# GEGLU feed-forward block: the order of the first fetches on two issue queues, and the place of ScalarE's table load

## Chip, cores and metric

The kernel runs on one core of one Trainium2 chip. The metric is the device time of one execution in microseconds (us). Before the change the median of three runs is 273.84 us (273.46 to 274.38).

## What is computed

```python
# x (32, 32, 1024); w_gate, w_up (1024, 3584); w_down (3584, 1024); all bfloat16
def reference(x, w_gate, w_up, w_down):
    return (_gelu(x @ w_gate) * (x @ w_up)) @ w_down      # gelu in its tanh form
```

With the first two dimensions of x joined there are 1024 tokens of width 1024, and 3584 hidden columns.

## The kernel before

Both matrix stages use one level of a Strassen scheme (its Winograd form). The operands are cut into two by two blocks, and seven block products replace eight, at the price of sums of blocks on VectorE and GpSimd. In the first stage the four blocks on one side are the upper and the lower 512 rows of `w_gate` (a11, a12) and of `w_up` (a21, a22). On the other side stand four blocks of x transposed: b11 and b21 (width rows 0 to 511 and 512 to 1023, tokens 0 to 511), b12 and b22 (the same rows, tokens 512 to 1023). Hidden columns are done in tiles of 128, and each product of a tile with 512 tokens is four matmuls, one for each 128 rows of width.

One of the seven products, a12 times b21, needs no sums. It is therefore computed ahead for the first 24 hidden tiles, in six groups of four tiles (group 0 to 5), and its results are copied to SBUF (`ahead`). While this runs, the rest of x and the first blocks of the weights arrive. This change concerns what groups 0 and 1 read.

**Transposed x.** Rows 0 and 1 of b21 (a row here is 128 rows of width) do not come from a transposing DMA. They are fetched untransposed into `x_nat`, as two blocks of 128 columns of x for all 512 tokens: x's first block (L199, on SyncE's queue) and x's second block (L218, on ScalarE's queue). TensorE transposes each block (`transposed`, L263, four transposes), and VectorE copies the result from PSUM into b21 (L271). Rows 2 and 3 of b21 come from a DMA transpose (L222, in `load_xT`). A one-element copy on GpSimd (L221), which reads x's first block and writes into rows 2 and 3, holds that transpose until x's first block has landed.

**Gate rows.** `load_ahead(i, k0, k1, eng)` (L204) fetches rows k0 to k1-1 of a12 for group i, 128 KB a row, on SyncE's queue unless ScalarE's is named. So "gate row k of group i" is one [128 x 512] block of `w_gate`.

**Order on TensorE** (written out by hand in the source): six warm-up products on constants (L254); four transposes of x's first block; seven short filler products on constants (L275); gate row 0 of group 0 (eight matmuls of 256 tokens, `by_halves(0)`); four transposes of x's second block; row 0 of group 1 for three tiles; row 1 of group 0 (`by_halves(1)`); row 1 of group 1 and the rest of its row 0; rows 2 and 3 of group 0 (L345 to L348); rows 2 and 3 of group 1; then groups 2 to 5, between which the first real products of the main loop begin.

**Order on the issue queues.** SyncE issues, in this order: x's first block; row 0 of group 0; row 0 of group 1; rows 2 and 3 of group 0 in one fetch; the transpose for b21 (after L221); rows 2 and 3 of group 1; two fetches for group 2; one for group 3; then w_up, w_gate, group 4, and the transposes of b11, b12 and, after group 5, b22. ScalarE issues: a small `probe` fetch (L202); x's second block; row 1 of group 0; row 1 of group 1. Behind them stands a one-column Gelu (L250), whose result nobody reads. It makes ScalarE load its table early. ScalarE's next work after that is the first copy of an `ahead` tile (L348).

The program has eight completion semaphores for these fetches, which it takes in turn. The ninth fetch in the program's order therefore waits until the first has landed, and so on.

Of the kernel before, what the change touches and what calls it, by code (L numbers as in the profile page):

```python
# [8 lines left out]
ACT = mybir.ActivationFunctionType  # L9
# [4 lines left out]
def kernel(  # L14
# [20 lines left out]
    nc = tc.nc  # L35
    P = nc.NUM_PARTITIONS
    fp32 = mybir.dt.float32
    f32r = mybir.dt.float32r
    bf16 = mybir.dt.bfloat16
# [7 lines left out]
    NB = 512  # L47
    assert N == 2 * NB and D == 2 * NB and F % (4 * P) == 0
    DT, FT = D // P, F // P
    KD = DT // 2  # L50
# [4 lines left out]
    KQ = DT // 4  # L55
# [19 lines left out]
    ework = one.enter_context(tc.tile_pool(name="ework", bufs=2))  # L75
# [62 lines left out]
    def load_w_all(ci, which):  # L138

        alloc_w(ci, which)  # L140
        load_w(nc.sync, ci, which, 0, KD if which == 0 and a12_stays(ci) else DT)
# [42 lines left out]
    ident = xpool.tile([P, P], bf16, name="ident")  # L184
# [6 lines left out]
    with tc.manual_schedule():  # L191
        def load_nat(eng, dt, p0, p1):
            eng.dma_start(
                out=x_nat[:, p0:p1, dt * P : (dt + 1) * P],
                in_=xf[p0 * P : p1 * P, (KD + dt) * P : (KD + dt + 1) * P].rearrange("(b p) d -> p b d", p=P),
            )
# [7 lines left out]
        def load_ahead(i, k0, k1, eng=nc.sync, j0=0, j1=KB):  # L204
            f0 = i * KB
            eng.dma_start(
                out=a12_ahead[i][:, k0:k1, j0 * P : j1 * P],
                in_=wg_r[:, KD + k0 : KD + k1, (f0 + j0) * P : (f0 + j1) * P],
            )

        def load_xT(nb, d0, d1):
            t = ((b11, b12), (b21, b22))[d0 // KD][nb]
            nc.sync.dma_start_transpose(
                out=t[:, d0 % KD : (d1 - 1) % KD + 1, :], in_=xf[nb * NB : (nb + 1) * NB, d0 * P : d1 * P]
            )

        load_ahead(0, 0, 1)
        load_nat(nc.scalar, 1, 0, NB_P)  # L218
        load_ahead(1, 0, 1)
        load_ahead(0, KQ, KD)  # L220
        nc.gpsimd.tensor_copy(b21[:1, KQ, :1], x_nat[:1, 0, :1])  # L221
        load_xT(0, KD + KQ, DT)  # L222
        load_ahead(0, 1, KQ, nc.scalar)
        load_ahead(1, 1, KQ, nc.scalar)
        a12_ahead += [spool.tile([P, KD, KB * P], bf16, name="a12b", tag=t) for t in ("s2", "s4", "s1", "s3")]
        load_ahead(1, KQ, KD)
        def load_halves(i):
# [12 lines left out]
        load_xT(1, KD, DT)  # L240
        for which in (1, 0):
            load_w_all(1, which)

        def gelu(src, tag, bufs):
            h = ework.tile([P, NB], bf16, name=tag, tag=tag, bufs=bufs)[:, : src.shape[-1]]
            nc.scalar.activation(h, src, ACT.Gelu_apprx_tanh)  # L246
            return h


        gelu(ident[:, :1], "h0", 6)  # L250

        warm_ps = acc("A")
        for _ in range(NWARM):
# [63 lines left out]
        def first_product(ft):  # L317
            psa = acc("A")
            prod(psa, quads(*chunk_of(ft))[0], b11, True)
            if ft < NAHEAD:  # L320
                return psa, gelu(added(ahead_at[ft], psa), "h0", 6)
            return psa, snap(psa, "sn1", 4)
# [38 lines left out]
        tt(t2, b22, t1, SUB)  # L361
        group_ahead(5, "CCAA", between=lambda: nc.scalar.copy(b22r, b22))
        begun = {ft: (psa, gelu(c, "h0", 6)) for ft, (psa, c) in begun.items()}
        tt(t3, b22, b12, SUB)
        next(chunk0)
# [8 lines left out]
        for ci in range(NCH):  # L374
# [8 lines left out]
            sn5, sn2, h1, h0 = [], [], [], []  # L383
# [17 lines left out]
            if fts[-1] < NAHEAD:  # L401
                h0 = first
# [228 lines left out]
```

## Time and profile before

| | us |
|---|---|
| median of three runs | 273.84 (273.46 to 274.38) |
| the profiled execution | 273.33 |
| its span, first to last instruction | 271.4 |
| the rest of it, around the span | 1.93 |
| TensorE busy in the span | 268.0 |
| ScalarE busy in the span | 115.4 |
| VectorE busy in the span | 204.0 |

Engines in the profile are PE (TensorE matmul), PEld (TensorE weight load), DVE (VectorE), ACT (ScalarE), POOL (GpSimd) and SP (SyncE); a name with a q at its end, such as ACTq, is an engine's instruction stream where it issues transfers. A row of the timeline gives the start and the length in us, the engine, the source line, the operation, the tile written and the tiles read, the number of instructions merged into the row, and in brackets the idle time before it with what ended it. Matmuls overlap, and their ends are modelled, so the step from one start to the next tells more than a length. A row of the list of transfers gives what is fetched, the issuing engine, the number, the size, and the time from the start of the issue until the transfer has landed.

### The profile page before, as it was taken

The numbers are of one execution on the slowest core, as the hardware profiler recorded it, in microseconds if no ns is written. First come the engines' busy times: TensorE is split into PE (matmuls) and PEld (weight loads), VectorE is DVE, ScalarE is ACT, GpSimd is POOL, SyncE is SP. The second block draws the span as 40 slices with busy tenths as digits, with TensorE's granted clock in tenths as the row PEclk, the third lists the DMA queues.
The fourth block names the chain that finished last, engine by engine and source line by source line (L and its number), as shares of the span: only waits on it lengthen the run. The fifth ranks groups of instructions, "written<-read, shape, count | busy, mean of one in ns | idle before, by whom it ended". The sixth has DMA issues, their size and how long they took to land.

```text
span 271.4 us, 3431 instructions
## 1 busy us (share of the span) xinstructions
PE 268.0 (99%) x1219; PEld 193.7 (71%) x1219; DVE 204.0 (75%) x205; ACT 115.4 (43%) x189; POOL 120.8 (45%) x61
## 2 busy tenths in 40 slices
PE   8999999999999999999999999999999999999996
PEld 5544776886787788688688687764458888888884
DVE  1447999986976877887777478469999999988711
ACT  2435756545644653645636535434000307870000
POOL 1080089997994994995995996000000000000000
PEclk9999999999999999999999999999999999999999
DMA  7999321514505505415234190005981537875111
GB/s 193 316 209 228 100 62 56 157 35 119 157 0 155 156 2 155 126 28 157 73 84 119 47 331 8 0 2 178 356 279 60 156 115 248 269 194 181 52 64 60
DMA packets 56657, 35.88 MB, mean 132 GB/s; under 512 B 10048, under 2 KB 56640, under 8 KB 56640
## 3 DMA queue, kind: packets, MB, share of 16 engines
q1 hardware_dynamic: 53232, 33.17, 43.3%
q10 hardware_dynamic: 3408, 2.49, 2.9%
q8 instruction: 10, 0.16, 0.3%
q14 instruction: 7, 0.06, 0.1%
HBM read 31.72 MB, written 2.10 MB: 125 GB/s over the span
## 4 chain that ended last, share of the span: by engine, by line
PE 99%; DVE 0%; issue 0%
PE psA L279 38%; PE psA L435 24%; PE psC L279 19%; PE psC L435 7%; PE psA L290 5%; PE psC L290 3%; PE psC L599 1%; PE psA L254 1%; PE psA L275 0%; PE tp L266 0%; DVE o_last L600 0%
## 5 line engine op out<-in xcount | busy, mean ns | idle before, releaser
L279 PE MATMUL psA<-t,s 128*128 128x512 f32 x224 | 57.2, 397 | 0.0
L246 ACT ACTIVATE h<-c 128x512 bf16<-128x512 f32 x56 | 34.4, 629 | 41.5 <-DVE c L309 41.5
L279 PEld LDWEIGHTS psA<-t,s 128*128 128x128 f32 x224 | 42.1, 188 | 9.5
L165 POOL TENSOR_TENSOR s<-wu 128x1024 fp32r<-128x1024 bf16 x13 | 29.5, 2271 | 28.0 <-DMA wu<-in_w_up_dram 24.0
L166 POOL TENSOR_TENSOR s<-s,wg 128x1024 fp32r<-128x1024 f32 x14 | 32.0, 2285 | 15.2 <-PE psA L279 14.2
L279 PE MATMUL psA<-b,wg 128*128 128x512 bf16 x128 | 29.4, 380 | 0.0
L168 POOL TENSOR_TENSOR s<-wg,wu 128x1024 fp32r<-128x1024 bf16 x13 | 28.9, 2219 | 0.0
L279 PE MATMUL psA<-t,a22r 128*128 128x512 f32 x112 | 27.9, 391 | 0.0
L279 PE MATMUL psC<-t,s 128*128 128x512 f32 x112 | 27.9, 391 | 0.0
L279 PE MATMUL psC<-b22r,s 128*128 128x512 f32 x112 | 27.7, 389 | 0.0
L309 DVE TENSOR_TENSOR c<-sn,psA 128x512 f32<-128x512 f32 x32 | 21.8, 682 | 6.7 <-PE psA L279 6.1
L314 ACT COPY sn<-psC 128x512 f32<-128x512 f32 x28 | 16.3, 588 | 22.8 <-PE psC L279 14.9
L279 PEld LDWEIGHTS psC<-t,s 128*128 128x128 f32 x112 | 21.0, 188 | 4.5
L279 PEld LDWEIGHTS psA<-t,a22r 128*128 128x128 f32 x112 | 21.0, 188 | 4.5
L279 PEld LDWEIGHTS psC<-b22r,s 128*128 128x128 f32 x112 | 21.0, 188 | 4.4
L309 DVE TENSOR_TENSOR c<-sn,psC 128x512 f32<-128x512 f32 x28 | 19.0, 686 | 6.0 <-PE psC L279 6.0
L412 DVE TENSOR_TENSOR lo<-c,h 128x512 bf16<-128x512 f32 x14 | 22.5, 1605 | 0.9
L279 PEld LDWEIGHTS <-wg 128*128 128x128 bf16 x128 | 11.8, 98 | 15.3 <-issue 2.4
L167 POOL TENSOR_TENSOR s<-wg,s 128x1024 fp32r<-128x1024 bf16 x10 | 21.6, 2160 | 0.8
L314 ACT COPY sn<-psA 128x512 f32<-128x512 f32 x32 | 18.3, 592 | 4.9 <-PE psA L279 4.6
L309 DVE TENSOR_TENSOR c<-ahead,psA 128x512 f32<-128x512 f32 x24 | 16.4, 686 | 3.5 <-PE psA L279 2.1
L412 DVE TENSOR_TENSOR hi<-c,h 128x512 bf16<-128x512 f32 x14 | 17.6, 1257 | 0.9
(88 smaller groups left out, 375.5 us busy)
## 6 DMA issues: line engine op xcount, KB each, us to landing
wu<-in_w_up_dram SPq DMA_DIRECT2D x14, 512.0 KB, 4.1
wdb<-in_w_down_dram SPq DMA_DIRECT2D x12, 512.0 KB, 4.8
wg<-in_w_gate_dram SPq DMA_DIRECT2D x10, 512.0 KB, 5.3
wdb<-in_w_down_dram SPq DMA_DIRECT2D x12, 384.0 KB, 4.5
v<-in_w_down_dram SPq DMA_DIRECT2D x4, 512.0 KB, 6.1
out_dram<-o_sb ACTq DMA_DIRECT2D x15, 128.0 KB, 1.7
v<-in_w_down_dram SPq DMA_DIRECT2D x4, 384.0 KB, 7.5
a12b<-in_w_gate_dram SPq DMA_DIRECT2D x4, 256.0 KB, 4.2
```

Source lines behind the costliest of these rows:

```text
L165: yield engs[0].tensor_tensor(s1, a21, a22, ADD)
L166: yield engs[1].tensor_tensor(s2, s1, a11, SUB)
L167: yield engs[2].tensor_tensor(s4, a12, s2, SUB)
L168: yield engs[3].tensor_tensor(s3, a11, a21, SUB)
L246: nc.scalar.activation(h, src, ACT.Gelu_apprx_tanh)
L254: nc.tensor.matmul(warm_ps, lhsT=ones_w, rhs=ones_m, start=True, stop=True)
L279: nc.tensor.matmul(ps, lhsT=lhs[:, k, :], rhs=rhs[:, k, :], start=(start and k == 0), stop=(k == KD - 1), skip_group_check=True,)
L290: nc.tensor.matmul(ps[:, cols], lhsT=a12_ahead[i][:, k, j * P : (j + 1) * P], rhs=b21[:, k, cols], start=(k == 0 and not cols.start), stop ...
L309: tt(t, s, ps, ADD)
L314: nc.scalar.copy(t, ps)
L412: tt(g_of(ft)[:, NB:], added(sn5[fl], psa[fl]), h1[fl], MUL)
L435: nc.tensor.matmul(banks[m], lhsT=lhs(k)[:, m * P : (m + 1) * P], rhs=rhs(k), start=(start and k == 0), stop=(k == HF - 1), skip_group_che ...
```

## The change

The dummy Gelu with its table load moves up on ScalarE, to stand between the probe and x's second block. Row 1 of group 0 moves from ScalarE's queue to SyncE's, ahead of the transpose for b21. Rows 2 and 3 of group 0 move from SyncE's queue to the end of ScalarE's. SyncE's first three fetches stay where they were.

```diff
         load_nat(nc.sync, 0, 0, NB_P)
         nc.scalar.dma_start(out=probe, in_=wg_r[::4, KD:, :2])
...
+        def gelu(src, tag, bufs):
+            h = ework.tile([P, NB], bf16, name=tag, tag=tag, bufs=bufs)[:, : src.shape[-1]]
+            nc.scalar.activation(h, src, ACT.Gelu_apprx_tanh)
+            return h
+
+        gelu(ident[:, :1], "h0", 6)
         load_ahead(0, 0, 1)
+        load_ahead(1, 0, 1)
         load_nat(nc.scalar, 1, 0, NB_P)
-        load_ahead(1, 0, 1)
-        load_ahead(0, KQ, KD)
+        load_ahead(0, 1, KQ)
+        load_ahead(1, 1, KQ, nc.scalar)
+        load_ahead(0, KQ, KD, nc.scalar)
         nc.gpsimd.tensor_copy(b21[:1, KQ, :1], x_nat[:1, 0, :1])
         load_xT(0, KD + KQ, DT)
-        load_ahead(0, 1, KQ, nc.scalar)
-        load_ahead(1, 1, KQ, nc.scalar)
...
-        def gelu(src, tag, bufs):
-            h = ework.tile([P, NB], bf16, name=tag, tag=tag, bufs=bufs)[:, : src.shape[-1]]
-            nc.scalar.activation(h, src, ACT.Gelu_apprx_tanh)
-            return h
-
-
-        gelu(ident[:, :1], "h0", 6)
```

In the built program the order of instructions on TensorE, VectorE and GpSimd is the same as before. On ScalarE the order is now: probe, table load, dummy Gelu (it waits for GpSimd's `ident`), x's second block, row 1 of group 1, rows 2 and 3 of group 0. Since the semaphores are taken in turn, the fetch of row 1 of group 1 now also waits until x's first block has landed, and the fetch of rows 2 and 3 of group 0 until row 0 of group 1 has landed. On SyncE the first `w_up` fetch now waits for the landing of the b21 transpose (before: of row 0 of group 1), and the `w_gate` fetch behind it for rows 2 and 3 of group 1 (before: row 1 of group 1).

## The prediction

> **What bounds the kernel now.** I read first the busy times and the chain that ended last, then TensorE's timeline of the first 14 us, then the fetches' landing times, and last the waits up to 60 us.
>
> ```profile
> PE 268.0 (99%) x1219; PEld 193.7 (71%) x1219; DVE 204.0 (75%) x205; ACT 115.4 (43%) x189; POOL 120.8 (45%) x61
> ...
> PE 99%; DVE 0%; issue 0%
> ```
>
> The span is 271.4 us. TensorE is busy for 268.0 of it, and 99% of the chain is TensorE's. In the waits of TensorE up to 14 us one row stands, the 0.8 us before its first product; from 12 to 60 us there is none of its matmul stream. So the change can gain only where TensorE's order itself gets shorter, and it touches none of TensorE's instructions. It can lose wherever a fetch lands after TensorE needs it. The work is to set landing times beside times of need.
>
> TensorE's timeline and its weight loads:
>
> ```profile
> 0.77 2.72 PE L254 MATMUL psA<-const-bfloat16-1.0 128*128 128x512 bf16 x6 [0.77 <-PEq L615]
> 3.23 0.42 PEld L266 LDWEIGHTS <-x_nat 128*128 128x128 bf16 x4 [0.64 <-DMA x_nat<-in_x_dram]
> 4.35 1.29 PEld L290 LDWEIGHTS <-a12a 128*128 128x128 bf16 x8
> 5.31 0.40 PE L290 MATMUL psC<-b,a12a 128*128 128x256 bf16 x2
> 5.66 0.32 PEld L266 LDWEIGHTS <-x_nat 128*128 128x128 bf16 x4
> 5.99 0.81 PE L290 MATMUL psA<-b,a12a 128*128 128x512 bf16 x3
> 6.64 0.38 PE L290 MATMUL psC<-b,a12a 128*128 128x256 bf16 x2
> 8.59 1.03 PE L290 MATMUL psC<-b,a12a 128*128 128x512 bf16 x4
> ```
>
> Times of need, a weight load standing 0.1 to 0.2 us ahead of its matmul: x's first block 3.23; row 0 of group 0 4.35; x's second block 5.66; row 0 of group 1 5.9; row 1 of group 0 6.5; row 1 of group 1 7.3 (four products of 0.22 us after 6.64, less the load); rows 2 and 3 of group 0, with the b21 transpose, about 8.4.
>
> ScalarE's timeline, then five transfers:
>
> ```profile
> 0.73 0.44 ACTq L202 DMA_DIRECT2D probe<-in_w_gate_dram  x1
> 1.20 0.45 ACTq L193 DMA_DIRECT2D x_nat<-in_x_dram  x1
> 1.69 1.01 ACTq L206 DMA_DIRECT2D a12a<-in_w_gate_dram  x2
> 2.73 1.28 ACT L246 ACT_TABLE_LOAD   x1 [2.73 <-issue]
> 4.02 0.21 ACT L246 ACTIVATE h<-ident 128x1 bf16<-128x1 bf16 x1
> 9.22 0.58 ACT L348 COPY ahead<-psC 128x512 f32<-128x512 f32 x1 [5.00 <-PE psC L290]
> ```
> ```profile
> x_nat<-in_x_dram SPq DMA_DIRECT2D x1, 128.0 KB, 2.4
> x_nat<-in_x_dram ACTq DMA_DIRECT2D x1, 128.0 KB, 3.3
> a12a<-in_w_gate_dram SPq DMA_DIRECT2D x1, 128.0 KB, 3.1
> a12a<-in_w_gate_dram SPq DMA_DIRECT2D x1, 256.0 KB, 4.2
> b<-in_x_dram SPq DMA_TRANSPOSE x1, 4.1
> ```
>
> Start of issue plus these times gives the landings of before: x's first block 0.74 + 2.4 = 3.1; its second 1.20 + 3.3 = 4.5; row 0 of group 0 1.24 + 3.1 = 4.3; row 0 of group 1 1.80 + 3.8 = 5.6; row 1 of group 0 1.69 + 3.7 = 5.4; row 1 of group 1 2.24 + 3.7 = 5.9; rows 2 and 3 of group 0 2.27 + 4.2 = 6.5; the transpose 3.44 + 4.1 = 7.5; rows 2 and 3 of group 1 4.83 + 4.2 = 9.0 (needed about 10.2). All are in time. Tightest are row 0 of group 0 (4.3 for 4.35) and row 0 of group 1 (5.6 for 5.9).
>
> **The change, part by part.**
>
> *Table load ahead of x's second block.* ScalarE ends the probe's issue at 1.17. Table load 1.28 and dummy Gelu 0.21 (its input `ident` is ready at 1.30, by GpSimd's rows) give 1.20 + 1.28 + 0.21 = 2.69. The second block is then issued at 2.70 instead of 1.20, 1.50 later. Its flight lies between 2.4 (the first block, nothing ahead of it) and 3.3 (the second, beside three fetches): landing at 5.1 to 6.0, against a need at 5.66. The stall is 0 to 0.34 us. I take the middle by bytes. In slices of 0.3 us, transfers begin at 1.8 to 2.1, some 1.2 after the first issue, and from 3.0 to 5.7 the core moves 283 to 372 GB/s. Some 3.9 is thus when data of the second block can start. By then SyncE's three gate rows ahead (131 KB each, 0.4 us apiece at 310 GB/s, from 2.7) are nearly through. The first block took 0.75 us for its bytes (155 and 240 GB/s in its main slices) and landed 0.4 after them: 3.9 + 0.75 + 0.4 = 5.1, with a share given to the neighbours 5.4. **Stall: 0.**
>
> The Trainium skill, "ScalarE: Activation LUTs", section "What ACT_TABLE_LOAD costs", speaks against this edit: it counts a drain of about 1.38 us to each table load of 1.28. The trace agrees with the load (1.28); between it and the work around it only 0.01 to 0.03 us stand. By the page the second block would be issued at about 4.1, which is the third rival.
>
> *Gate rows of both groups on SyncE.* SyncE's issues at 0.74, 1.24 and 1.80 stay. The fourth, at 2.27, becomes row 1 of group 0 (0.58 later than from ScalarE). With ScalarE's three fetches gone from the start, each row passes fewer bytes: row 0 of group 0 has 131 KB fewer ahead, 0.4 us, so it lands near 3.9; row 0 of group 1 near 4.3; row 1 of group 0 near 4.7 (5.5 by its old flight of 3.7 less 0.4), for 6.5. Their gain is nothing here: the seven fillers hold TensorE until about 4.4 whatever lands. Row 1 of group 1 is issued at about 3.2 (behind the second block, when x's first has landed at 3.1) and lands, with its old 3.7, at 6.9 at the latest, for 7.3. **Sum 0.** The DMA transpose still waits for L221 at 3.44, so its issue does not move.
>
> *Rows 2 and 3 of group 0, last on ScalarE.* They now wait for row 0 of group 1, at 4.3 (5.6 at worst, its old landing). Nothing is queued behind them on ScalarE until the copy at 9.22. Issued at 4.3, with data from 5.5, they share the engines with the transpose and with rows 2 and 3 of group 1 (issued 4.83). At half of some 280 GB/s, 262 KB take 1.9 us, plus 0.4: 7.8. Upper bound: last of the three, they land where rows 2 and 3 of group 1 land now, 9.0, or a little after, at 9.2. Need 8.4, so the price is 0 to 0.8 us; by the flight of the same size now, 4.3 + 4.2 = 8.5, it is 0.1. I take **0**, being nearer to the shared case: bytes issued ahead are 1.05 MB with the transpose, fewer than the 1.31 MB that now land by 7.5.
>
> The Trainium skill, "DMA: Bandwidth & Descriptors", section "Issuing engines are not separate DMA queues", says that fetches of all issuing engines run on the same 16 engines and interleave, so that a second queue saves only issue time. By it the fetch takes the 4.2 of its neighbours, 8.5, and the sum would be 0.1 more.
>
> *Later fetches.* `w_up` waits for the transpose (about 7.2 instead of an issue at 6.99), `w_gate` for rows 2 and 3 of group 1 (about 9.0; its issue now runs from 7.53 to 9.23). Both stand behind 1.5 MB still to be moved, 5 us at 300 GB/s, so the engines do not starve. The nearest need is b22: landed at 25.9, its sum on VectorE ends at 28.25 and TensorE uses it from 29.6. That spare 1.35 us covers what shift is left, at most 0.5.
>
> **Sum.** 273.33 + 0 + 0 + 0 = 273.33 against the profiled execution. This one lies 0.5 us below the median of the runs; on the median the forecast is **273.8 us, no change**. What a measurement of this kernel can tell from no change is about 0.3%, 0.8 us.
>
> **Rivals.**
>
> 1. *Late fetches* (22%). The second block takes 3.3 (0.3 us), or rows 2 and 3 of group 0 fall behind the transpose (0.1 to 0.8). For it: needs 5.66 and 8.4 lie inside both ranges. Against: fewer bytes in front. Time 274.1 to 274.6, both together 274.9.
>
> 2. *A gain from spare time* (12%). Row 0 of group 0 now lands with 0.05 us to spare, so runs in which it is late stall and the new order frees them: 273.84 to 273.46 are the median and the fastest run, so about 0.4, 273.4; with the other tight row up to 272.9. Against: the profiled execution has no such stall.
>
> 3. *Slower: ScalarE's queue is held longer* (10%). Place: between the dummy Gelu and the second block's issue. What follows a Gelu at once there is not shown before, as ScalarE's next work comes at 9.22. Each us by which the issue passes 5.66 - 2.4 = 3.26 is a us of stall at 5.66; from 4.1 on it exceeds 0.8 us and decides. An issue at 4.1 lands at 6.5 to 7.4: +0.8 to +1.7, 274.6 to 275.6. Against: near the end an output is issued 0.03 us after ScalarE's cast of it.
>
> 4. *A stall keeps TensorE slow* (4%). Products of 256 tokens start about 0.21 us apart up to 5.31 and 0.11 after, while the page's granted clock reads 9 in every slice. If a stall at 5.66 put this step off, each further us of slow stretch costs half a us: 274.4 to 275.0. The Trainium skill, "TensorE: Matmul & The Clock Gate", Part 1, has such a gate with a free-running window; that its phase differs by run fits the spread of 0.9 us.
>
> 5. *The change does less than it says*: two of SyncE's rows stood there already, and only row 1 of group 0 joins them. That gives the forecast's own time.
>
> **Chances and range.** Forecast 52%, rivals 22, 12, 10 and 4. Beyond 0.3% slower (over 274.66) lie most of rival 3, half of rival 4 and a fifth of rival 1: 15%. Faster than 273.02: a third of rival 2 and the runs' spread, 7%. Within: 78%. The range, 273.0 to 274.9, takes in the unknown prices of rival 1 and most of rival 2, and leaves out the rest of rivals 3 and 4.
>
> **What the changed profile would show.** ScalarE's table load at 1.2, x's second block issued at 2.7 and landed by 5.6; the weight loads of L266's second row with no idle time that a DMA ended; rows 2 and 3 of group 0 issued near 4.3 and landed before 8.4; TensorE's share still 99%. A wait of TensorE for `x_nat` or `a12a` between 5 and 9 us would prove me wrong by its length, and an issue of the second block after 3.3 would be rival 3.

## The result

The changed kernel takes 275.06 us (median of 22 executions, 273.38 to 277.05) against 273.56 us for the kernel before (22 executions, 272.76 to 274.38). The ratio is 1.0064, with a 95% interval from 1.0048 to 1.0080. It is slower, by about 1.5 us, where no change was forecast, and the median lies above the range given. The profiled execution of the changed kernel took 275.14 us, with a span of 273.3 us: 1.9 us more than the span of before.

In the page, TensorE has lost its hold on the chain:

```profile
PE 268.9 (98%) x1219; PEld 193.9 (71%) x1219; DVE 202.7 (74%) x205; ACT 115.9 (42%) x189; POOL 119.5 (44%) x61
...
PE 95%; DMA 3%; SPq 0%; DVE 0%; issue 0%
```

The chain in order of time, from the start up to 16 us (start, length, what), says which transfers stand in it:

```profile
1.24 0.51 SPq L206
1.75 0.05 issue
1.80 3.44 DMA a12a<-in_w_gate_dram
5.24 0.02 issue
5.26 5.12 DMA a12a<-in_w_gate_dram
10.38 0.05 issue
10.43 1.04 PE psC L288 x4
```

The first transfer is row 0 of group 1, from SyncE's queue. The second is rows 2 and 3 of group 0, issued 0.02 us after the first has landed. TensorE starts on them 0.05 us after they have landed. So one fetch waits for another, and TensorE waits for the second. Its timeline and ScalarE's (line numbers are two lower than before) show the same from the engines:

```profile
5.39 0.63 PE L288 MATMUL psC<-b,a12a 128*128 128x256 bf16 x2
6.25 0.63 PE L264 MATMUL tp<-ident,x_nat 128*128 128x128 bf16 x4
7.37 0.38 PE L288 MATMUL psC<-b,a12a 128*128 128x256 bf16 x2
10.43 1.04 PE L288 MATMUL psC<-b,a12a 128*128 128x512 bf16 x4 [0.94 <-DMA a12a<-in_w_gate_dram]
```
```profile
1.21 1.28 ACT L219 ACT_TABLE_LOAD   x1 [1.21 <-PEq L613]
1.34 0.41 ACTq L193 DMA_DIRECT2D x_nat<-in_x_dram  x1
2.51 0.21 ACT L219 ACTIVATE h<-ident 128x1 bf16<-128x1 bf16 x1
3.21 2.43 ACTq L206 DMA_DIRECT2D a12a<-in_w_gate_dram  x2
```

Rows 2 and 3 of group 0 are begun at 10.43 instead of 8.59. That is 1.84 us, nearly all of the 1.9 us. Not all of it is the wait. In this execution the products ahead of them ran later too, because TensorE's slow first stretch (products of 256 tokens 0.21 us apart) lasted longer than before. Without the wait these rows would have begun near 9.3, an estimate: 1.30 us after the product at 8.03, as before after the one at 7.29. So the wait cost about 1.1 us here, and the rest of the 1.84 is the slower start. With a faster start TensorE would have waited longer, as the landing at 10.4 sets when it goes on.

The second block of x was issued at 1.34, while the table load ran from 1.21 to 2.49: the load did not hold it. What did take time is in the last row, where ScalarE's two gate fetches spread over 2.43 us instead of 1.01.

The flights, from the list of transfers, in the order x's second block, row 0 of group 1, row 1 of group 1, the transpose, rows 2 and 3 of group 0:

```profile
x_nat<-in_x_dram ACTq DMA_DIRECT2D x1, 128.0 KB, 3.6
a12a<-in_w_gate_dram SPq DMA_DIRECT2D x1, 128.0 KB, 3.4
a12a<-in_w_gate_dram ACTq DMA_DIRECT2D x1, 128.0 KB, 3.8
b<-in_x_dram SPq DMA_TRANSPOSE x1, 4.6
a12a<-in_w_gate_dram ACTq DMA_DIRECT2D x1, 256.0 KB, 5.1
```

Landings: 1.34 + 3.6 = 4.9, 1.80 + 3.4 = 5.2, 3.21 + 3.8 = 7.0, 3.45 + 4.6 = 8.1, and 5.26 + 5.1 = 10.4. These are in time but for the last. Row 0 of group 0 landed at 1.24 + 3.3 = 4.5, a little late: TensorE's weight load waited 0.17 us for it, and the first product began at 4.57 instead of 4.46.

### The profile page after: what moved, and what is told of

Its sections match the earlier page's. It is cut to its first block, busy times and chain, and to the rows that moved or that the text cites. A ratio compares the mean times of both kernels' runs of the same rounds, so it can differ in the third digit from the quotient of the medians.

```text
span 273.3 us, 3430 instructions
## 1 busy us (share of the span) xinstructions
PE 268.9 (98%) x1219; PEld 193.9 (71%) x1219; DVE 202.7 (74%) x205; ACT 115.9 (42%) x189; POOL 119.5 (44%) x61
## 4 chain that ended last, share of the span: by engine, by line
PE 95%; DMA 3%; SPq 0%; DVE 0%; issue 0%
PE psA L277 38%; PE psA L433 24%; PE psC L277 19%; PE psC L433 7%; PE psA L288 4%; DMA a12a<-in_w_gate_dram 3%; PE psC L288 2%; PE psC L597 1%; SPq L206 0%; SPq L193 0%; DVE o_last L598 0%
## 5 line engine op out<-in xcount | busy, mean ns | idle before, releaser
L165 POOL TENSOR_TENSOR s<-wu 128x1024 fp32r<-128x1024 bf16 x13 | 28.6, 2202 | 31.1 <-DMA wu<-in_w_up_dram 26.8
L410 DVE TENSOR_TENSOR lo<-c,h 128x512 bf16<-128x512 f32 x14 | 20.7, 1479 | 0.9
```

The lines of the kernel that those rows point to most:

```text
L165: yield engs[0].tensor_tensor(s1, a21, a22, ADD)
L410: tt(g_of(ft)[:, NB:], added(sn5[fl], psa[fl]), h1[fl], MUL)
```

## The experiments

The theory after the result, called W in the texts: the loss is the semaphore's turn. With the table load ahead of them, ScalarE's last fetches stand later in the built program's order of fetches, past the eighth. They then wait for the landing of an earlier fetch, and the one that lands too late stalls TensorE. Its rivals: T, the table load itself holds the fetches; R, the rows' new places on the queues cost the time.

**Each part alone.** *table_only* is the kernel before with the table load moved; *rows_only* is the changed kernel with it moved back:

```diff
 (rows_only, against the changed kernel)
-        gelu(ident[:, :1], "h0", 6)
         load_ahead(0, 0, 1)
...
         load_ahead(0, KQ, KD, nc.scalar)
+        gelu(ident[:, :1], "h0", 6)
```

> The kernel before with the table load and the dummy Gelu moved ahead of x's second block, and the fetches of gate rows as they were. In the built program the semaphores then fall so that row 1 of group 0 waits for the landing of x's first block and row 1 of group 1, ScalarE's last fetch, for that of row 0 of group 1. Theory W (the wait for a semaphore's turn delays a fetch, and that stalls TensorE): row 1 of group 1 is issued near 5.2, lands near 9 and is needed at 7.3, so a stall of 1.5 to 2 us and a time 1.2 to 2.2 us above before; x's second block is issued at 1.3 as in the changed kernel. Theory T (the table load itself holds ScalarE's fetches): the stall is at the transposes of x's second block, and the time is up to 1.5 us above before. Theory R (the rows' new places on the queues are the cost): no difference, within 0.3 us.

> The changed kernel with the table load and the dummy Gelu put back behind ScalarE's last fetch: the rows stand in their new places, and no fetch on ScalarE's queue waits for a semaphore. Theory W: rows 2 and 3 of group 0 are issued near 2.2 and land by 7.5, no stall near 8.5, and the time is within 0.4 us of before. Theory T: the same, within 0.3 us of before. Theory R: the full loss of the changed kernel, 1.5 us above before.

table_only: 275.07 us against 273.42 for before, ratio 1.0065 (1.0050 to 1.0081). rows_only: 273.66, ratio 1.0004 (0.9991 to 1.0017). So the table load carries the whole loss and the rows none, and R falls. But the table load does its harm by the wait. In table_only x's second block was again issued at 1.34 and TensorE did not wait for it. It waited for row 1 of group 1, 1.43 us:

```profile
1.34 0.40 ACTq L193 DMA_DIRECT2D x_nat<-in_x_dram  x1
3.26 2.04 ACTq L206 DMA_DIRECT2D a12a<-in_w_gate_dram  x2
...
9.17 1.25 PE L289 MATMUL psA<-b,a12a 128*128 128x512 bf16 x5 [1.43 <-DMA a12a<-in_w_gate_dram]
```

This fetch was issued at 4.92, where row 0 of group 1 had landed, and flew 4.2 us. In rows_only, where none waits, ScalarE issued its two gate fetches from 1.78 on, rows 2 and 3 of group 0 landed at 2.34 + 4.7 = 7.0, and their products began without idle time at 9.03:

```profile
9.03 1.03 PE L288 MATMUL psC<-b,a12a 128*128 128x512 bf16 x4
```

**The wait alone.** *rows_wait* leaves the table load behind and adds the wait by other means, a one-element copy whose result the fetch then overwrites (against rows_only; the copy that holds the transpose also moves up, to stand ahead of it):

```diff
+        nc.gpsimd.tensor_copy(a12_ahead[0][:1, KQ, :1], a12_ahead[1][:1, 0, :1])
         load_ahead(0, KQ, KD, nc.scalar)
         gelu(ident[:, :1], "h0", 6)
```

> The kernel rows_only with one addition: a one-element copy on GpSimd, behind the one that holds the transpose, from row 0 of group 1 into row 2 of group 0, so that the fetch of rows 2 and 3 of group 0 on ScalarE's queue waits until row 0 of group 1 has landed, as it does in the changed kernel, with the table load still behind. Theory W: the issue falls to 5.2 to 5.7, the fetch lands near 10, TensorE stalls 1 to 1.6 us there, and the time is 1.0 to 1.8 us above before. Theory T: no difference from before, within 0.3 us. Theory R: 1.5 us above before with and without this wait.

275.1 us, ratio 1.0088 (1.0055 to 1.0122). Three of its seven executions had the lower clock that is treated further down; the median of the other four is 274.9. In the profiled one, the fastest of the seven: issue at 4.99, flight 4.6, stall 1.05 us:

```profile
9.72 1.02 PE L289 MATMUL psC<-b,a12a 128*128 128x512 bf16 x4 [1.05 <-DMA a12a<-in_w_gate_dram]
```

The wait without the table load ahead gives the loss, and T falls.

**Less of the wait.** In *short_wait* one fetch is taken out of the turn (`load_halves(2)` becomes `load_ahead(2, 0, KD)` in the changed kernel), so the same fetch waits for an earlier landing.

> The changed kernel with group 2 fetched in one transfer instead of two. That takes one fetch out of the semaphores' turn, so that rows 2 and 3 of group 0 wait for row 0 of group 0 (landed at 4.5 in the changed kernel) instead of row 0 of group 1 (5.2). Theory W: issue at 4.6 instead of 5.26, the stall near 8.5 is shorter by 0.5 to 0.9 us, and the time is 0.6 to 1.1 us above before instead of 1.5. Theories T and R: unchanged, 1.5 us above before.

274.6 us, ratio 1.0050 (1.0033 to 1.0067). The issue moved from 5.26 to 4.20, right behind the landing of row 0 of group 0 (1.24 + 2.9 = 4.1), and with a flight of 5.2 us the landing moved from 10.4 to 9.4. TensorE went on at 9.46 instead of 10.43. The stall fell less, from 0.94 to 0.72 us, because TensorE also reached the wait sooner in this execution. The direction is W's. The time, 1.2 us above before, lies a little over the range expected, and the interval of the changed kernel's ratio overlaps this one, so the gain itself is not clear of the noise.

**The late issue that the forecast had assumed.** *rows23_sp* puts rows 2 and 3 of group 0 back on SyncE (`nc.scalar` taken off that line of the changed kernel); *table_free2* also leaves out the probe fetch, which takes one more out of the turn.

> The changed kernel with rows 2 and 3 of group 0 back on SyncE's queue, behind row 1 of group 0 and ahead of the transpose. The semaphores' turn then makes x's second block wait for the probe's landing (2.6) and row 1 of group 1 for row 0 of group 0 (about 4.3). So this run has, at last, the late issue of x's second block on which the forecast was worked out. Theory W (waits for a semaphore's turn): second block issued at 2.65, row 1 of group 1 at 4.4, landing near 8.1 for a need at 7.3, stall 0.5 to 1.0 us, time 0.5 to 1.2 us above before. If the forecast's flight is right, the second block lands at 5.1 to 5.4 and row 0 of group 1 near 4.3, with no stall at the transposes; if its upper bound is right, at 6.0 with a stall of 0.3. Rival (the fetch of rows 2 and 3 on ScalarE is the only harm): within 0.3 us of before.

> As rows23_sp and without the probe fetch, whose data nobody reads. One fetch fewer: x's second block waits for nothing, though it stands behind the table load, and row 1 of group 1 waits for row 0 of group 0. Theory W: second block issued by 1.3, no stall there; row 1 of group 1 issued near 4.2, landing near 7.9, stall 0.3 to 0.8 us, time 0.3 to 0.9 us above before. Theory T (the table load holds ScalarE's fetches): second block issued after 2.0 and a stall at the transposes.

rows23_sp: 275.48 us, ratio 1.0082 (1.0061 to 1.0102). The second block was issued at 2.67, right behind the probe's landing (0.73 + 1.9 = 2.6), flew 4.3 us and landed at 7.0. That the table load and the dummy Gelu end at about the same time is chance, as table_free2 shows. TensorE waited for the second block:

```profile
7.00 0.40 PE L264 MATMUL tp<-ident,x_nat 128*128 128x128 bf16 x4 [0.63 <-DMA x_nat<-in_x_dram]
```

So the flight of the forecast's first step (2.4 to 3.3 us) would probably have been too short as well, had the issue been late. The test is not exact, since rows 2 and 3 of group 0, issued on SyncE at 2.74, shared the transfer engines here. Row 0 of group 1 landed at 1.80 + 2.8 = 4.6, not 5.6. The time rose by 2.15 us, more than the 0.5 to 1.2 expected. The profiled execution is the fastest of the six (274.55); one of the others had the lower clock, and what the rest lost beyond the 0.63 us was not traced.

table_free2: 274.86 us, ratio 1.0053 (1.0037 to 1.0068). The second block was issued at 1.34 and caused no wait. Row 1 of group 1, waiting for row 0 of group 0, went out at 4.10, landed at 9.1, 1.2 us later than I expected, and stalled TensorE by 2.14 us. The expected range, 0.3 to 0.9 us, was missed: the time rose by 1.5. It rose less than the stall, because TensorE's faster stretch began early in the profiled execution (its filler products took 0.71 us instead of 0.95): it reached the wait sooner, and waited longer.

**What makes the flight long.** *wait_alone* holds group 2's fetches, and all behind them on SyncE, until the late fetch has landed (one line added to rows_wait: `nc.gpsimd.tensor_copy(a12_ahead[2][:1, 0, :1], a12_ahead[0][:1, KQ, :1])` ahead of `load_halves(2)`).

> The kernel rows_wait with the fetches of group 2 and all behind them on SyncE held until rows 2 and 3 of group 0 have landed (a one-element copy on GpSimd), so that this fetch shares the transfer engines only with the transpose and rows 2 and 3 of group 1. Theory Q (its long flight, 4.6 to 5.1 us for 256 KB, is the share it gets beside a backlog on SyncE's queue): flight 3.3 to 3.8 us instead of 4.6, landing near 8.5, stall there 0 to 0.5 us; a new stall may come at group 2, whose fetch is issued about 3 us later. Rival (the flight is set by the transpose or by the fetch itself): flight 4.4 us or more.

The flight was 3.6 us, as Q said; in the three traced executions of rows_wait (two of them below) it is 4.6, 5.6 and 5.8. The stall was 0.75 us, above the 0 to 0.5 expected, because row 0 of group 1 landed later here and the fetch went out at 5.52. The time, 276.54 us (ratio 1.0119, 1.0105 to 1.0132), is worse, since the transfers then stood still from 8.7 to 10.2 us and the later groups came late (TensorE's products waited 1.2 us for `a12b`). So the late fetch loses 1 us or more to the backlog beside it. What is left over an undisturbed flight (2.4 us for half the bytes) goes to the transpose and to rows 2 and 3 of group 1, which it still shares with; the two were not told apart.

**A longer stall, and TensorE's clock.** Five of the 22 executions of the changed kernel had a mean granted clock of 0.993 to 0.994 and took 276.8 to 277.1 us; the median of the other 17 is 274.87. Where the clock is on record for executions of the kernel before, of rows_only and of the two variants with fewer fillers below, none reads under 0.999. *long_wait* makes the stall longer: the copy reads the transposed `b21[:1, KQ, :1]` instead, behind the transpose.

> The kernel rows_wait with the hold on rows 2 and 3 of group 0 lengthened: the one-element copy on GpSimd now reads the transposed row 2 of b21, so the fetch waits until the transpose has landed (7.3 to 8.0). Theory W: issue at 7.7 to 8.3, landing at 12 to 13, stall 3.5 to 4.5 us, time 3.3 to 4.5 us above before. Theory C (beyond W: a stall of more than about a microsecond can also let TensorE's clock fall back, as the mean granted clock of 0.993 to 0.994 in some executions of the changed kernel and of rows_wait suggests): every execution shows a mean granted clock near 0.99, the products behind the stall start twice as far apart for a while, and the time is 5 to 6.5 us above before.

281.26 us, ratio 1.0288 (1.0273 to 1.0303), mean clock 0.988 in each of its four executions: 7.9 us above before, more than either theory expected. The flight grew to 7.6 us, the stall to 6.72 us. In these stages (length, busy time of each engine, then the granted clock, the share of the transfer engines and GB/s) the clock falls while TensorE waits, and the stall is followed by a stretch at half speed:

```profile
7.90:11.10 3.20, 0.53 (x3) 0.03 (x1) 0.00 (x0) 1.48 (x2) 0.00 (x0) 1.00 0.97 318
...
11.40:15.00 3.60, 0.00 (x0) 0.00 (x0) 0.00 (x0) 0.00 (x0) 0.10 (x1) 0.50 1.12 325
15.00:18.00 3.00, 2.63 (x6) 1.02 (x8) 0.69 (x1) 0.68 (x2) 2.92 (x2) 0.50 1.19 272
18.00:20.00 2.00, 2.00 (x11) 0.90 (x10) 1.37 (x2) 1.33 (x3) 1.92 (x2) 1.00 1.03 213
```

*rows_wait_b* and *rows_wait_c* are rows_wait once more, to see such an execution at the smaller stall.

> The kernel rows_wait once more, for the trace of an execution whose mean granted clock is near 0.994 (three of its seven executions had it, and five of 22 of the changed kernel). Theory C: where it is, a stretch of some 3.4 us at half the granted clock begins shortly after the stall for rows 2 and 3 of group 0, the products in it stand twice as far apart, and the time is near 277; where it is not, the time is near 274.8. Rival: the low clock lies elsewhere in the execution and has nothing to do with the stall.

> As rows_wait_b, a second chance of an execution with the lower mean clock.

Both had it: 277.26 us (mean clock 0.993) and 278.01 us (0.994), beside 273.38 for before. In rows_wait_c the stall was 2.88 us. In rows_wait_b the late fetch flew 5.6 us and the stall was 2.18 us:

```profile
10.85 1.02 PE L289 MATMUL psC<-b,a12a 128*128 128x512 bf16 x4 [2.18 <-DMA a12a<-in_w_gate_dram]
11.71 4.44 PE L289 MATMUL psA<-b,a12a 128*128 128x512 bf16 x12
```
```profile
11.00:12.00 1.00, 1.00 (x6) 0.46 (x5) 0.09 (x1) 0.52 (x1) 0.00 (x0) 0.99 1.09 364
12.00:13.00 1.00, 1.00 (x4) 0.34 (x3) 0.61 (x1) 0.52 (x2) 0.00 (x0) 0.50 1.17 323
...
14.00:15.00 1.00, 1.00 (x4) 0.43 (x3) 0.10 (x1) 0.59 (x1) 0.00 (x0) 0.50 1.12 315
15.00:16.00 1.00, 1.00 (x6) 0.37 (x5) 0.69 (x1) 0.24 (x1) 0.42 (x1) 0.81 1.39 322
```

The clock is 0.50 from about 12.0 to 15.4, and twelve products that took 2.75 us in the other execution took 4.44. So a stall of some two microseconds can cost 1.7 us more, after it has ended. It need not: in table_free2 the stall was 2.14 us, and the granted clock stayed at 1.00.

The records of the clock in the kept traces, from which the views take their means, hint at what decides. In rows_wait_b the first record begins at 5.14 us, where the products step to the faster rate, and the clock falls at 11.97, which is 6.83 us later. It is 6.83 us in rows_wait_c (5.03 to 11.85) and in long_wait (4.32 to 11.15) too. The low stretch lasts 3.41 us, in long_wait twice that. Counted from the step in pieces of 3.41 us, the piece that ended with the fall held 2.18, 2.88 and 2.72 us of TensorE's waiting. In table_free2 (step at 4.00) the wait lay across two pieces, 0.37 us in the first and 1.77 in the second. So it seems to be the waiting inside one such piece that counts, not the length of the stall alone. Four executions are few, and no run was made to test this.

**Do earlier rows gain anything?** *rows_fill3* and *before_fill3* are rows_only and before with `NFILL = 3` instead of 7.

> The kernel rows_only (rows in their new places, no waits) with three filler products instead of seven behind the first transposes. The forecast said that earlier gate rows gain nothing because the fillers hold TensorE until 4.4. If that is so, the first real product starts near 4.1 instead of 4.46 (row 0 of group 0 landed at 3.9 in rows_only), and the time is 0.1 to 0.4 us below rows_only and 0 to 0.3 us below before. Rival (row 0 of group 0 or VectorE's copy of the transposed block holds that product as well, or the pause delays TensorE's faster stretch): no gain, within 0.2 us of rows_only or above it.

> The kernel before with three filler products instead of seven. Row 0 of group 0 landed at 4.3 there, so the first real product can start at most 0.1 us earlier: the time is within 0.3 us of before, on either side. The rival as for rows_fill3: a pause of TensorE ahead of that product delays its faster stretch, and the time is 0.3 to 1 us above before.

rows_fill3: 273.68 us, ratio 1.0011 (0.9996 to 1.0026). before_fill3: 273.44, ratio 1.0001 (0.9982 to 1.0021). In rows_fill3 the first real product did start at 4.09 instead of 4.47, but no gain can be measured. In before_fill3 TensorE waited 0.35 us for row 0 of group 0 (begun at 4.59), so that row was indeed the tight one. No version tried beats the kernel before.

## Why the prediction was wrong

- *What bounds the kernel*: right. TensorE is the bound, and the change could only lose, where a fetch lands late.
- *Table load ahead of x's second block*: "The second block is then issued at 2.70" was wrong: it went out at 1.34. I added the durations of the engine's work (1.28 + 0.21) to the queue that issues transfers. The result, no stall there, came out right by luck, for another reason. Rival 3 falls with it: ScalarE was held by nothing at that place. The drain that the Trainium skill ("ScalarE: Activation LUTs", "What ACT_TABLE_LOAD costs") counts to a load is not seen either: the dummy Gelu starts at 2.51, 0.02 us behind the load.
- *Gate rows on SyncE*: no gain, as forecast. But row 0 of group 0 landed at 4.5, not "near 3.9", and cost 0.1 us. Row 0 of group 1 landed at 5.2, not "near 4.3". That the second block had not moved out of its way is part of it: with that block late, in rows23_sp, it landed at 4.6, and in the variants with it early at 4.8 to 5.3. This mattered, as it ends the wait of the next step. Row 1 of group 1 came as forecast (issued at 3.21, landed at 7.0 for 6.9).
- *Rows 2 and 3 of group 0, last on ScalarE* is the step that failed. The mechanism was named, a fetch that waits for row 0 of group 1 and may land after its need, but its price was put at 0, with 0.8 as the upper bound. Issue: 5.26 for 4.3, though a worst landing of 5.6 stood in the same sentence, from which no bound was worked out. Flight: 5.1 for 3.5. Landing: 10.4 for 7.8, with a need at 8.4 in the forecast and at 9.0 in this execution, whose slow stretch was longer. I had counted the bytes ahead, and not that a fetch which leaves three microseconds later meets a backlog: my sum let it share with the transpose and rows 2 and 3 of group 1, and left out group 2's fetches, which SyncE issued from 5.46 on. From 4.5 to 6.9 us the core moved 300 GB/s before and 139 after. Their busy share is much the same in the view (1.17 and 1.07), so the transfer engines did not stand idle, but rows 2 and 3 were hardly there to be moved. From 6.9 to 9.0 the core moved 0.66 MB, and ScalarE's queue had 0.25 of it. The Trainium skill ("DMA: Bandwidth & Descriptors", "Queues, rings and completion order") says that each transfer engine goes round between its queues packet by packet; wait_alone's 3.6 us against 4.6 agrees with a shared engine.
- *Later fetches*: right. `w_up` went out at 8.08 and `w_gate` at 9.45, somewhat later than forecast, and from 12 to 60 us no wait of TensorE's products stands in the profile.
- *Rivals*: rival 1 was the case that came, with its price too small (274.1 to 274.9 where 275.06 came). Rival 2 did not show: with three fillers instead of seven there was no gain. Rival 4 was right in that a stall can lower the clock, and wrong on how: not by putting off the first faster stretch, but by a new slow one after the stall. The first step to the faster rate came late, at 6.77 us, in the changed kernel, but also at 6.22 in rows_only, which has no stall.

## What to carry to other kernels

Moving an instruction can change which semaphore a later transfer waits for. Read the waits of the built program for each transfer that the move pushes back, and price them from the landing they wait for at its worst to a flight beside the backlog that will then stand there. A queue that issues transfers need not wait for the engine's work that stands ahead of it. A stall of TensorE need not be paid once its length is over: from about two microseconds on, reckon with a slow stretch behind it, which came here after stalls of 2.18 us and more, and not after one of 2.14.

## What the runs showed of the hardware

- ScalarE's queue issued a fetch at 1.34 us, while a table load that stands ahead of it in the program ran from 1.21 to 2.49.
- After a stall of 2.18 us the granted clock fell to 0.50 for some 3.4 us; after one of 2.14 us, in table_free2, it did not. The Trainium skill ("TensorE: Matmul & The Clock Gate", Part 1) gives a window of that length; it asks for about one idle window ahead of the fall, and here 2.18 us of waiting was enough.
- Where TensorE's products first step from 0.21 to 0.11 us apart, the views give the granted clock as 1.00 on both sides, but the records of the clock in the kept traces begin only at that step. It came at 4.00 us in table_free2, 5.33 before, 6.22 in rows_only and 6.77 in the changed kernel, with no tie to a stall.
